# The fourth batch's first Fourier stage as quarter-size matmuls on sums and differences, with a new order of down matmuls around it

## Chip, core and metric

The kernel runs on one core of a Trainium2 chip. The metric is device microseconds of one execution. Five engines matter here. TensorE (PE in the profile) does the matmuls, VectorE (DVE) and ScalarE (ACT) do elementwise work and empty the PSUM banks that PE writes. GpSimd (POOL) and SyncE (SP) issue transfers (DMAs). Each engine works through its own instructions strictly in the order in which the kernel issues them, so an instruction that waits holds up all that stands behind it on that engine.

## The reference

```python
# x (8, 3008, 256), filt_r, filt_i (1505, 256)
X = np.fft.rfft(x, axis=1)
Y = X * (filt_r + 1j * filt_i)[None]
y = np.fft.irfft(Y, n=3008, axis=1).reshape(24064, 256)
h = y @ w_in                                       # (256, 2048)
g = np.maximum(h, 0.0) + alpha * np.minimum(h, 0.0)
out = g @ w_out                                    # (2048, 256)
```

A filter is applied in the frequency domain along the sequence, for each of 256 channels, and its result goes through two dense layers with a leaky rectifier between them.

## The kernel before

**The dense part.** The 24064 tokens are cut into 48 blocks of 512 tokens (the sixth of every twelve has 384). `Block.up` (L572) does, for one slice j of 128 of the 2048 hidden features, two matmuls of 512 columns ("U" below) into a PSUM tile `hps`, of which there are two. Two slices share one `hps` tile, so ScalarE empties a tile after every second step (L586). VectorE then forms `m` for each of the two slices (L589), and after every fourth step adds it to `gtb` (L591). `Block.down` (L626) multiplies the result with `w_out` ("down" matmuls, "d", 256 columns each, L631), a unit of four matmuls at a time (three in a block of 384), one block later than the ups. The queue `units` holds the units that are still to do. A PSUM tile `op` (two of them) holds the sums of 256 tokens. ScalarE copies it out (L636) and SyncE stores it (L559).

**The Fourier part.** 3008 is 94 times 32, and a batch goes through four stages, each cut into pieces. They work in float16.
- First stage: `piece_a` (L177, "A") multiplies a 94-row tile `xs` of the input with the table `wf1` of 96 columns: two matmuls of 512 columns into an `hps` tile, which ScalarE copies to `asb` (L313). There are eight pieces for a batch. `save_a` (L187) writes each quarter to `a_dram`, and `turn_a` (L221) reads it back with the axes turned, as `at`, both on SyncE's queue.
- Batches 4 to 7 (counted from 0) use another form of it. `load_halves` (L130) loads the first and the second half of the rows as two tiles `lo` and `hi`. `less` (L192) puts their difference beside them, in rows 64 to 110 of `lo`, and `plus` (L196) then overwrites the first rows with their sum; both are single VectorE instructions. `piece_q` (L200, "Q") does the same transform with four matmuls of 47 rows by 64 columns in the four quarters of the array, since the even outputs need the sum alone and the odd ones the difference alone.
- Second stage: `piece_b` (L231, "B"), eight matmuls of 64 rows by 64 columns into the single PSUM tile `psF`. VectorE multiplies it with two filter tables (L245 `ww`, L246 `uu`), GpSimd shifts `ww` between partitions by DMA into `sw` (L252), and `piece_s` (L255, VectorE L257) adds `sw` to `uu`. Batch 1 adds in the DMA instead (L250).
- Third stage: `piece_c` (L259, "C"), eight matmuls on `uu`, into an `hps` tile. Then a turn through DRAM again (L274).
- Fourth stage: `pair_d` (L303, "D"), eight matmuls of 94 columns into `psF`, emptied by ScalarE (VectorE in batch 0) into `yT`, which the ups read.

Batch 0 is done ahead of all by a class of its own (`First`, L321); its last pieces overlap the first block.

**The order of the work** is written out by hand. A step is one `up` of two matmuls. Blocks are 16 steps long; the first stepped block begins at step 16. `put` and `put_h` (L642, L645) enter pieces in a table `plan` by step, and `psum` counts at each step how many of them take an `hps` tile. The loop (L742 to L763) issues at each step first some downs (`pop`), then the planned pieces, then the two ups, then mostly one more unit of downs. Before step 150 one unit is popped ahead of planned pieces, where there are any. From step 150 on as many units as there are `hps` pieces are popped ahead of them and as many again behind them, and some odd steps keep their unit back so that there are enough (L759).

In batch 2 the pieces B stand at steps 106, 116, 126, 136, 148 and 158, the additions (`piece_s`) seven steps later, and the pieces C at 116, 126, 136, 148, 158 and 172 (L706). Batch 3's pieces A stand at 106, 112, 118, 124, 130, 132, 140 and 144 (L711). Its input tiles are loaded at steps 57, 69, 113 and 123, from a pool of four `xs` tiles.

**The lines of the tables** that the prediction uses: L184 A matmuls, L210 Q matmuls, L238 B, L269 C, L291 D, L577 and L600 ups, L631 downs; L313 all of ScalarE's copies from the Fourier stages; L194 `less`, L198 `plus`.

Of the kernel before, what the change touches and what calls it, by code (L numbers as in the profile page):

```python
# [15 lines left out]
N2 = 32  # L16
NK = 24
D = 256
# [37 lines left out]
def kernel(  # L56
# [56 lines left out]
        return bass.AP(tensor=x.tensor, offset=x.offset + (b * NFFT + 8 * c) * D,  # L113
                       ap=[[N2 * D, N1], [1, 8 * D]])

    def load_x(b, c, held=False):
        xs = p_x.tile([128, 8 * D], FP16, name="xs")
        if held:
            for r in (slice(0, 32), slice(64, 96)):
                nc.vector.memset(xs[r, 0:2], 0.0)  # L120
        if b:
            for r in (slice(0, 48), slice(48, N1)):
                nc.gpsimd.dma_start(out=xs[r], in_=xrow(b, c)[r])  # L123
        else:
            w = 8 * D // (1 + (c == 3))
            for o in range(0, 8 * D, w):
                nc.gpsimd.dma_start(out=xs[0:N1, o : o + w], in_=xrow(b, c)[:, o : o + w])
        return xs
# [37 lines left out]
    class Fft:  # L166
# [107 lines left out]
        def turn_c(self, q):  # L274
            k = 8 * q
            for par in range(2):
                for c in range(2):
                    r = par * 48 + c * NK + k
                    p = par * 64 + c * N2
                    nc.sync.dma_start(  # L280
                        out=v_dram[self.b, r : r + 8].rearrange("k s d -> s k d"),
                        in_=self.v[p : p + N2, k : k + 8])
            if q == 2:
                for g in range(4):
                    s = slice(8 * g, 8 * g + 8)
                    nc.sync.dma_start(out=self.zt[:, s], in_=v_dram[self.b, :, s])

        def inverse(self, pd, g, dh, mh):
# [278 lines left out]
    class Block:  # L567
        def __init__(self, p, t0, tn):
            self.p, self.t0, self.tn = p, t0, tn
            self.gts, self.gs = [], []  # L570

        def up(self, j):  # L572
            tn = self.tn
# [40 lines left out]
                nc.vector.tensor_add(g, g, m)  # L614
                self.gts += [g[:, h] for h in range(4)]

        def start_down(self, last):
            n = self.tn // 128
            ends = [2, 3, 4] if last else list(range(2, n, 2)) + [n]
            half = 12 if last else 8  # L620
            self.todo = []
            for s0, s1 in zip([0] + ends, ends):
                for ks in (range(half), range(half, 16)):
                    self.todo += [(s0, s1, si, k) for si in range(s0, s1) for k in ks]

        def down(self, q):  # L626
            n = self.tn // 128
            for s0, s1, si, k in self.todo[n * q : n * (q + 1)]:
                if si == s0 and k == 0:
                    self.op = psO.tile([128, 2, D], FP32, name="op")  # L630
                nc.tensor.matmul(self.op[:, si - s0], self.gts[k][:, 128 * si : 128 * si + 128],  # L631
                                 wout_s[:, k], start=(si == s0 and k == 0), stop=(si == s1 - 1 and k == 15))
                if k == 15 and si == s1 - 1:
                    m = s1 - s0
                    osb = p_osb.tile([128, 2, D], FP32, name="osb")
                    nc.scalar.activation(osb[:, 0:m], self.op[:, 0:m], AF.Copy)  # L636
                    for lane in range(m):
                        store(self.p, self.t0 + 128 * (s0 + lane), osb, lane)

# [2 lines left out]
    def put(step, fn, *args):  # L642
        plan.setdefault(step, []).append((fn, args))
# [4 lines left out]

    def plan_fft(b, a_at, ta, x_at, b_at, add, c_at, d_at):
        f = Fft(b)  # L650
        split = b > 3
        for q in range(6):
            put_h(c_at[q], f.piece_c, q)
            if q % 2 == 1:
                put(c_at[q] + 1, f.turn_c, q // 2)
        for q in range(6):
            put(b_at[q], f.piece_b, q, not add)
            if add:
                put(b_at[q] + add, f.piece_s, q)
        for i in range(8):  # L660
            put_h(a_at[i], f.piece_q if split else f.piece_a, i)
        for c in range(4):
            put(a_at[2 * c + 1] + split, f.save_q if split else f.save_a, c)
            if b in (2, 3):
                put(x_at[c], lambda b=b, c=c: xc.update({(b, c): load_x(b, c, b == 3 and c > 1)}))
            if split:
                x0, x1, x2 = x_at[c]
                put(x0, lambda b=b, c=c: xc.update({(b, c): load_halves(b, c)}))
                put(x1, f.less, c)
                put(x2, f.plus, c)  # L670
        w = NK // len(ta)
        for q, t in enumerate(ta):
            put(t, f.turn_a, nc.sync, w * q, w * q + w)
        for i in range(8):
            put(d_at[i], f.pair_d, i, on_act)
# [5 lines left out]
        nc.vector.tensor_scalar(alm_s, al_s, 1.0, -1.0, OP.mult, OP.add)  # L681

    put(1, f0.half_d, 1, on_act, "o")
    put(1, f0.half_d, 3, on_dve, "o")
    put(1, f0.piece_t, 2, on_dve)
    for i in (6, 7):
        put(3, lambda i=i: on_dve(*f0.half_t(i, "o")))
    put(7, f0.pair_d, 2, on_dve)
    for g, ts, ds, te, de in ((2, (19, 23), (26, 29), (on_dve, on_dve), (on_dve, on_dve)),
                              (3, (32, 34), (36, 38), (on_act, on_act), (on_act, on_act))):  # L690
        for i in range(2):
            put(ts[i], f0.piece_t, 2 * g + i, te[i])
            put(ds[i], f0.pair_d, 2 * g + i, de[i])
# [7 lines left out]
    def d_steps(p):  # L701
# [1 line left out]

    plan_fft(1, range(16, 32, 2), [31] * 4, None, (40, 46, 52, 58, 63, 68), 0, (52, 58, 64, 70, 76, 80),
             (93, 95, 98, 101, 114, 121, 142, 154))
    plan_fft(2, (48, 54, 60, 66, 72, 74, 82, 84), [90] * 4, (32, 40, 50, 56),  # L706
             (106, 116, 126, 136, 148, 158), 7, (116, 126, 136, 148, 158, 172), d_steps(96))
    for b in range(3, NB):
        p = 96 * (b - 1)
        if b == 3:  # L710
            a_at = (106, 112, 118, 124, 130, 132, 140, 144)  # L711
            x_at = (57, 69, 113, 123)
            ta = (155, 166)
        else:
            a_at = [p - 96 + t for t in (-34, -22, 2, 2, 14, 26, 38, 50)]
            x_at = [[p - 96 + t for t in r] for r in
                    ((-66 if b == 4 else -68, -52, -40), (-32, -18, -10), (-20, -4, 8), (4, 20, 32))]
            ta = (p - 39, p - 28)
        plan_fft(b, a_at, ta, x_at, range(p + 2, p + 74, 12), 8, range(p + 14, p + 86, 12), d_steps(p))

# [9 lines left out]
    for step in range(16):  # L730
# [4 lines left out]
                     8: [lambda i=i: f0.half_d(i, on_dve, "o") for i in (6, 7)]}.get(step, []))  # L735
        for fn, args in plan.pop(step, ()):
            fn(*args)
    blk.start_down(False)
    units.extend((blk, q) for q in range(16))
    step = 16  # L740

    for p, t0, tn in blocks[1:]:  # L742
        blk = Block(p, t0, tn)
        for j in range(16):
            n = psum.get(step, 0)
            if step < 150:
                pop(1 if n else 0)
            else:
                pop(n)
            for fn, args in plan.pop(step, ()):  # L750
                fn(*args)
            if step >= 150:
                pop(n)
            blk.up(j)
            if n:
                last = step
            else:
                soon = any(t in psum for t in range(step + 1, step + 14))
                if not (step >= 150 and step % 2 and step - last > 2 and soon and len(units) < 18 - j):  # L759
                    pop(1)  # L760
            step += 1
        blk.start_down(step == 16 * len(blocks))
# [33 lines left out]
```

## Time and profile before

| what | value |
|---|---|
| median of three runs | 768.38 us (768.12 to 769.5) |
| the profiled execution | 768.86 us, of which the span of the core is 767.1 us |
| granted TensorE clock | 1.0 |
| PE busy | 756.9 us, 99% of the span |
| DVE busy | 633.9 us, 83% |
| ACT busy | 583.3 us, 76% |
| POOL busy | 147.0 us, 19% |

Matmuls overlap in the trace: a busy matmul lasts longer than the distance to the next one. So the busy time says little about where PE loses time. What counts is the distance from one start to the next. Two ups of 512 columns stand 0.216 us apart, two downs 0.109 us. A larger distance is a stall, even if the profile calls only part of it idle. A view of a stretch of time lists the instructions of an engine merged by line, with the start, the length and, in square brackets, the idle time ahead of them and who ended it.

Step 16 begins at 43.9 us of the span, step 40 at 70.8, step 70 at 102.8, step 98 at 130.1, step 106 at 136.9, step 116 at 146.7, step 136 at 167.4 and step 158 at 188.6 (found by counting the U matmuls of the trace).

### The profile page before, as it was taken

The page shows a single profiled execution, that of the slowest core. Times are in us where ns is not written, and L with a number is a line of the kernel's source. Part 1 is how long each engine was busy: PE and PEld are TensorE (multiplying, and loading weights), DVE is VectorE, ACT ScalarE, POOL GpSimd, SP SyncE. Part 2 cuts the span into 40 slices and gives each one's busy share as a digit, 9 for nine tenths or more (in the row PEclk, how much of TensorE's full clock was granted, in tenths as well). Part 3 has the DMA queues.
Part 4 walks back from the last instruction along what each step waited for, and adds up shares of the span by engine and source line. Part 5 has one row for each costly group of instructions (what it writes and reads, how often), then busy time and mean ns, then how long its engine had stood idle before and what let it go on. Part 6 is the DMA issues. An engine that isn't in the chain of part 4 may idle for free.

```text
span 767.1 us, 16602 instructions
## 1 busy us (share of the span) xinstructions
PE 756.9 (99%) x6553; PEld 507.3 (66%) x6553; DVE 633.9 (83%) x1163; ACT 583.3 (76%) x672; POOL 147.0 (19%) x277
## 2 busy tenths in 40 slices
PE   8999999999999999999999999999999999999998
PEld 4666657666666666666666666766666666766666
DVE  4898975889889998899978998999877888666663
ACT  4788788888778777887778787787777777776664
POOL 6610840221211220121202122022101212000000
PEclk9999999999999999999999999999999999999999
DMA  9996996665752559533774438544463223510111
GB/s 162 157 225 173 175 204 181 166 171 139 178 153 69 139 142 197 143 97 97 188 205 96 125 104 179 166 97 118 131 162 87 71 68 97 152 36 28 42 42 56
DMA packets 97486, 100.04 MB, mean 130 GB/s; under 512 B 12086, under 2 KB 83398, under 8 KB 97216
## 3 DMA queue, kind: packets, MB, share of 16 engines
q1 hardware_dynamic: 82384, 69.50, 31.1%
q0 software_dynamic: 15024, 29.49, 21.4%
q8 instruction: 51, 0.84, 0.4%
q14 instruction: 27, 0.22, 0.1%
HBM read 55.02 MB, written 46.66 MB: 133 GB/s over the span
## 4 chain that ended last, share of the span: by engine, by line
PE 91%; DMA 4%; POOL 2%; DVE 1%; ACT 1%; issue 1%; SPq 0%; POOLq 0%; DVEq 0%; ACTq 0%
PE op L631 41%; PE hps L577 40%; PE psF L291 3%; PE hps L269 2%; PE psF L238 1%; PE hps L184 1%; DMA xs<-in_x_dram 1%; DMA uu<-ww 1%; PE hps L210 1%; DMA a_dram<-asb 1%; PE hps L600 1%; POOL filt_s L147 1%; DMA filt_s<-in_filt_r_dram 1%; POOL uu L250 1%; ACT asb L313 0%
## 5 line engine op out<-in xcount | busy, mean ns | idle before, releaser
L586 ACT ACTIVATE gtb<-hps 128x1024 f16<-128x1024 f32 (+1 forms) x376 | 377.9, 1007 | 132.6 <-PE hps L577 129.7
L631 PE MATMUL op<-wout_s,gtb 128*128 128x256 f16 x3008 | 431.1, 273 | 0.6 <-DVE gtb L614 0.6
L577 PE MATMUL hps<-yT,win_s 128*128 128x512 f16 (+1 forms) x1504 | 418.1, 375 | 0.3 <-ACT asb L313 0.2
L631 PEld LDWEIGHTS <-gtb 128*128 128x128 f16 x3008 | 290.8, 98 | 164.8 <-issue 10.7
L589 DVE TENSOR_SCALAR m<-gtb,alm_s 128x512 f16<-128x512 f16 (+1 forms) x752 | 227.3, 346 | 97.6 <-ACT gtb L586 96.1
L591 DVE TENSOR_TENSOR gtb<-gtb,m 128x2048 f16<-128x2048 f16 (+1 forms) x188 | 226.1, 1203 | 10.4
L577 PEld LDWEIGHTS <-win_s 128*128 128x128 f16 x1504 | 142.5, 98 | 54.9 <-issue 5.3
L252 POOL DMA_DIRECT2D sw<-ww x144 | 71.8, 506 | 414.2 <-DVE ww L245 399.4
L636 ACT ACTIVATE osb<-op 128x512 f32<-128x512 f32 (+1 forms) x97 | 56.6, 583 | 12.3 <-PE op L631 10.9
L313 ACT ACTIVATE asb<-hps 128x1024 f16<-128x1024 f32 (+1 forms) x56 | 56.7, 1020 | 6.4 <-PE hps L184 4.8
L245 DVE TENSOR_TENSOR ww<-psF,filts_s 128x1024 f16<-128x1024 f32 x42 | 51.2, 1219 | 1.0 <-DMA uu<-ww 0.7
L313 ACT ACTIVATE v<-hps 128x1024 f16<-128x1024 f32 (+1 forms) x43 | 43.5, 1012 | 11.2 <-PE hps L269 11.1
L246 DVE TENSOR_TENSOR uu<-psF,filt_s 128x1024 f16<-128x1024 f32 x42 | 51.1, 1216 | 0.0
L313 ACT ACTIVATE yT<-psF 128x752 f16<-128x752 f32 (+1 forms) x59 | 46.5, 788 | 1.7 <-PE psF L291 1.5
L291 PEld LDWEIGHTS <-zt 96*128 96x128 f16 x504 | 28.0, 98 | 5.8 <-issue 0.4
L291 PE MATMUL psF<-wi_s,zt 96*128 96x94 f16 x448 | 27.9, 205 | 0.0
L257 DVE TENSOR_TENSOR uu<-uu,sw 128x1024 f16<-128x1024 f16 x36 | 24.6, 683 | 1.3 <-DMA sw<-ww 1.3
L250 POOL DMA_DIRECT2D uu<-ww x24 | 19.6, 1174 | 28.1 <-DVE uu L246 21.4
L123 POOL DMA_DIRECT2D xs<-in_x_dram x24 | 17.6, 1009 | 12.9 <-DMA win_s<-in_moe_w_in_dram 4.5
L194 DVE TENSOR_TENSOR xs<-xs 47x2048 f16<-47x2048 f16 x16 | 19.5, 1219 | 0.4
L198 DVE TENSOR_TENSOR xs<-xs 47x2048 f16<-47x2048 f16 x16 | 19.4, 1210 | 0.0
L269 PE MATMUL hps<-uu,twi_s 64*64 64x256 f16 x336 | 17.6, 281 | 0.2 <-DMA uu<-ww 0.2
(99 smaller groups left out, 264.8 us busy)
## 6 DMA issues: line engine op xcount, KB each, us to landing
out_dram<-osb SPq DMA_DIRECT2D x128, 128.0 KB
v_dram<-v SPq DMA_DIRECT2D x84, 128.0 KB
zt<-v_dram SPq DMA_DIRECT2D x28, 384.0 KB
sw<-ww POOLq DMA_DIRECT2D x144, 64.0 KB, 2.7
xs<-in_x_dram POOLq DMA_DIRECT2D x40, 192.0 KB, 6.6
at<-a_dram SPq DMA_DIRECT2D x40, 192.0 KB
a_dram<-asb SPq DMA_DIRECT2D x32, 192.0 KB
a_dram<-asb SPq DMA_DIRECT2D x12, 384.0 KB
```

Of the source, the lines that this page charges most:

```text
L245: nc.vector.tensor_mul(ww, px, fs)
L246: nc.vector.tensor_mul(uu, px, f)
L252: nc.gpsimd.dma_start(out=sw[o : o + 32], in_=ww[i : i + 32])
L269: nc.tensor.matmul(ps[64 * par : 64 * par + 64, e, 256 * h : 256 * h + 256], twi_s[r, 4 * q + 2 * h + par], u[r, par, h], start=True, stop ...
L291: nc.tensor.matmul(ps[:, m], self.zt[:, 8 * g + 4 * mh + m, dh * 128 : dh * 128 + 128], self.wi, start=True, stop=True)
L313: nc.scalar.activation(o, i, AF.Copy)
L577: nc.tensor.matmul(self.hps[:, j % 2, 0:tn], win_s[:, kt, j * 128 : (j + 1) * 128], yT[:, kt, self.t0 : self.t0 + tn], start=(kt == 0), st ...
L586: nc.scalar.activation(g[:, 2 * i : 2 * i + 2], self.hps[:, :, 0:tn], AF.Copy)
L589: nc.vector.tensor_scalar(m[:, 2 * i + h], g[:, 2 * i + h], 0.0, a, OP.min, OP.mult)
L591: nc.vector.tensor_add(g, g, m)
L631: nc.tensor.matmul(self.op[:, si - s0], self.gts[k][:, 128 * si : 128 * si + 128], wout_s[:, k], start=(si == s0 and k == 0), stop=(si == ...
L636: nc.scalar.activation(osb[:, 0:m], self.op[:, 0:m], AF.Copy)
```

## The change

- Batch 3 joins batches 4 to 7 in the quartered first stage (`split = b > 2`). Its pieces Q stand at steps 98, 98, 106, 106, 116, 126, 136 and 148. For each of the four input tiles the load, `less` and `plus` stand at (69, 80, 86), (91, 98, 102), (99, 108, 112) and (107, 122, 130). The two small memsets of the earlier loads go.
- The rule of downs on both sides of the planned pieces holds from step 96 on rather than 150.
- The first stepped block's downs (of block 0) go by quarters of k: the first four k of all four token groups, then the next four, so that two `op` tiles are open at once. At step 16 no unit is popped ahead of the piece, at step 24 two are.
- In batch 0 the turn `whole_t(2)` is issued on PE ahead of `half_d(3)` and emptied behind it; the second of the turns of group 2 moves from step 23 to 24 and the two D pieces of that group from 26 and 29 to 27 and 30.
- Batch 2's loads are entered at steps 39, 45, 51, 57 rather than 32, 40, 50, 56, and batch 4's first load one step later. Batch 3's `zt` is read in eight transfers rather than four.

In the order of issue, GpSimd's queue changes only by batch 3's loads: its first one no longer stands ahead of the transfers of batch 1's fourth piece B (step 58), and the two first ones now stand behind those of the sixth (step 68).

```diff
-    def load_x(b, c, held=False):
+    def load_x(b, c):
         xs = p_x.tile([128, 8 * D], FP16, name="xs")
-        if held:
-            for r in (slice(0, 32), slice(64, 96)):
-                nc.vector.memset(xs[r, 0:2], 0.0)
...
             if q == 2:
-                for g in range(4):
-                    s = slice(8 * g, 8 * g + 8)
+                w = 4 if self.b == 3 else 8
+                for g in range(0, N2, w):
+                    s = slice(g, g + w)
                     nc.sync.dma_start(out=self.zt[:, s], in_=v_dram[self.b, :, s])
...
-        def start_down(self, last):
+        def start_down(self, last, quarters=False):
             n = self.tn // 128
+            if quarters:
+                self.todo = [(s0, s0 + 2, si, k) for k0 in range(0, 16, 4) for s0 in range(0, n, 2)
+                             for si in (s0, s0 + 1) for k in range(k0, k0 + 4)]
+                return
...
-        split = b > 3
+        split = b > 2
...
-            if b in (2, 3):
-                put(x_at[c], lambda b=b, c=c: xc.update({(b, c): load_x(b, c, b == 3 and c > 1)}))
+            if b == 2:
+                put(x_at[c], lambda b=b, c=c: xc.update({(b, c): load_x(b, c)}))
...
     put(1, f0.half_d, 1, on_act, "o")
+    put(1, lambda: later.append(f0.whole_t(2)))
     put(1, f0.half_d, 3, on_dve, "o")
-    put(1, f0.piece_t, 2, on_dve)
+    put(1, lambda: on_dve(*later.pop()))
...
-    for g, ts, ds, te, de in ((2, (19, 23), (26, 29), (on_dve, on_dve), (on_dve, on_dve)),
+    for g, ts, ds, te, de in ((2, (19, 24), (27, 30), (on_dve, on_dve), (on_dve, on_dve)),
...
-    plan_fft(2, (48, 54, 60, 66, 72, 74, 82, 84), [90] * 4, (32, 40, 50, 56),
+    plan_fft(2, (48, 54, 60, 66, 72, 74, 82, 84), [90] * 4, (39, 45, 51, 57),
...
-            a_at = (106, 112, 118, 124, 130, 132, 140, 144)
-            x_at = (57, 69, 113, 123)
+            a_at = (98, 98, 106, 106, 116, 126, 136, 148)
+            x_at = ((69, 80, 86), (91, 98, 102), (99, 108, 112), (107, 122, 130))
...
-                    ((-66 if b == 4 else -68, -52, -40), (-32, -18, -10), (-20, -4, 8), (4, 20, 32))]
+                    ((-65 if b == 4 else -68, -52, -40), (-32, -18, -10), (-20, -4, 8), (4, 20, 32))]
...
-    blk.start_down(False)
+    blk.start_down(False, True)
...
-            if step < 150:
-                pop(1 if n else 0)
+            if step < 96:
+                pop({16: 0, 24: 2}.get(step, 1 if n else 0))
...
-            if step >= 150:
+            if step >= 96:
                 pop(n)
...
-                if not (step >= 150 and step % 2 and step - last > 2 and soon and len(units) < 18 - j):
+                if not (step >= 96 and step % 2 and step - last > 2 and soon and len(units) < 18 - j):
                     pop(1)
```

In `down`, `self.op` becomes a table by `s0`, so that both open tiles are found.

## The prediction

> **What bounds the kernel now.** I read the page's busy row first, then PE's waits, then the distances from start to start of PE's matmuls.
>
> ```profile
> PE 756.9 (99%) x6553; PEld 507.3 (66%) x6553; DVE 633.9 (83%) x1163; ACT 583.3 (76%) x672; POOL 147.0 (19%) x277
> ```
>
> ```profile
> PE op L631 <- DVE gtb L614: 0.6, 2, 0.4
> PE psF L238 <- DMA at<-a_dram: 0.2, 1, 0.2
> PE hps L269 <- DMA uu<-ww: 0.2, 1, 0.2
> ```
>
> PE is the bound. Its waits are few, and longer than listed, since a busy matmul is drawn longer than its share: the C piece at step 70 starts at 103.79 and goes on at 104.31, a stall of 0.51 us where the list says 0.2. Summed by distances, PE stalls some 9.6 us in the run, 6.0 of them ahead of 45 us, and 0.3 in four places between steps 106 and 146. So a change gains by less PE work or by these stalls, and loses by each new one.
>
> **The change, part by part.** Times are of the profiled execution. Ahead of step 98 I count gains as a shift of all engines.
>
> *PE work.* Two stretches of PE's timeline, with C and B alone and with Q behind them:
>
> ```profile
> 147.61 0.41 PE L269 MATMUL hps<-uu,twi_s 64*64 64x256 f16 x8
> 147.86 0.39 PE L238 MATMUL psF<-at,twf_s 64*64 64x256 f16 x8
> 148.18 1.04 PE L577 MATMUL hps<-yT,win_s 128*128 128x512 f16 x4
> ```
>
> ```profile
> 190.01 0.41 PE L269 MATMUL hps<-uu,twi_s 64*64 64x256 f16 x8
> 190.26 0.39 PE L238 MATMUL psF<-at,twf_s 64*64 64x256 f16 x8
> 190.47 0.39 PE L210 MATMUL hps<-xs,wfq_s 47*64 47x512 f16 x4
> 190.79 1.05 PE L631 MATMUL op<-wout_s,gtb 128*128 128x256 f16 x8
> ```
>
> From C to what follows takes 0.57 us without Q and 0.78 with it: Q costs 0.21 to 0.22 in such a burst. A costs 0.43 (172.45 to 172.88 at step 140). Six Q stand behind B: 6 x 0.22 = 1.31 less. The two at step 98 stand alone and pay for entering and leaving the small tiles, 0.09 each: the last down stands 0.20 ahead of C at 190.01, not 0.109. So 0.87 becomes 0.62. Sum: **-1.56**. The four stalls between 106 and 146 go with A: **-0.30**.
>
> [...]
>
> *Start.* At 33.64 PE waits 0.49 for an `op` tile (`half_d(3)`); the eight turn matmuls, 0.45, go into that hole, so PE and ScalarE run 0.44 earlier. Before, downs wait for `gtb` at 43.05 (0.38) and 45.36 (0.56). With no unit at step 16, A follows the last up4 at 42.23, but the ups wait for `hps`, which ScalarE empties until 43.45: 0.8 lost. The downs at 44.37 need the first quarter alone, ready at 42.55. A of step 18 then starts at 45.24 instead of 46.25, with one unit (0.44) owed: 0.57 ahead. At step 27 D arrives at 56.15, and the `zt` copy, now behind an add in VectorE's queue, ends at 56.35: 0.25 back. **-0.32**, between 0 and -0.57.
>
> *Step 70.* GpSimd issues batch 3's first loads at 92.03 and 92.53, between `ww` and the shifts for that C; the last shift is issued at 96.15 and takes 8.1 us, against 5.5 for the median. Without them the stall goes: **-0.50**, between 0 and that. The 0.52 at 71.30 stays: those reads follow `asb` of step 30, which only moves along.
>
> *ScalarE at steps 98 to 106.* This is how two Q in a row look, at step 290:
>
> ```profile
> 314.35 0.60 PE L210 MATMUL hps<-xs,wfq_s 47*64 47x512 f16 x8
> 314.79 1.94 ACT L313 ACTIVATE asb<-hps 128x1024 f16<-128x1024 f32 x2 [0.15 <-PE hps L210]
> 314.88 0.83 PE L631 MATMUL op<-wout_s,gtb 128*128 128x256 f16 x6
> 315.86 1.02 PE L577 MATMUL hps<-yT,win_s 128*128 128x512 f16 x4 [0.15 <-ACT asb L313]
> ```
>
> Q fills an `hps` tile in 0.22, ScalarE needs 0.92 from one to the next, and six downs (0.65) don't cover the rest: the up at 315.86 is 0.31 late. Step 98 has the same with D ahead, whose copy (0.70) goes first: with the step beginning at 130.10, the copy starts at 131.23, `asb` at 131.93, ends at 132.95, and the ups wait from 132.38 to 133.00: 0.62. ScalarE's backlog, with D's copy of step 101, delays the ups of 104 by 0.31 and, behind an `osb` copy, those of 106 by 0.50. **+1.43**, between 0.6 (twice 0.31) and 1.8.
>
> [...]
>
> *VectorE, steps 106 to 136.* Here is its queue in the same stretch, before:
>
> ```profile
> 138.98 1.22 DVE L245 TENSOR_TENSOR ww<-psF,filts_s 128x1024 f16<-128x1024 f32 x1
> 140.11 1.22 DVE L246 TENSOR_TENSOR uu<-psF,filt_s 128x1024 f16<-128x1024 f32 x1
> 141.24 0.63 DVE L589 TENSOR_SCALAR m<-gtb,alm_s 128x512 f16<-128x512 f16 x2
> 141.91 1.22 DVE L591 TENSOR_TENSOR gtb<-gtb,m 128x2048 f16<-128x2048 f16 x1
> 143.05 1.26 DVE L589 TENSOR_SCALAR m<-gtb,alm_s 128x512 f16<-128x512 f16 x4
> 144.35 1.23 DVE L591 TENSOR_TENSOR gtb<-gtb,m 128x2048 f16<-128x2048 f16 x1
> 145.49 0.68 DVE L257 TENSOR_TENSOR uu<-uu,sw 128x1024 f16<-128x1024 f16 x1
> ```
>
> It has no gap from B's products (step 106) to the addition of step 113, which C of step 116 needs: the addition ends at 146.17, C starts at 147.52. The margin is 1.35. The change puts `less` of step 108 and `plus` of 112 ahead of that addition: 1.14 us each from start to start (later batches' rows of L194 and L198), 2.28. Followed through from step 98: VectorE idles until 135.08, when ScalarE delivers the late `gtb` of steps 98 and 99; then products, adds and `plus` of 102 put `ww` at 141.15; 2.26 for `ww` and `uu`, 1.8, `less` 1.14, 2.43, `plus` 1.13 and the addition's 0.68 end at 150.6. PE reaches C at 148.55, since it too lost 1.43. **+2.1**. The ten steps up to 126 add one `less` and VectorE just keeps up (addition at 160.5, C at 160.7). Up to 136 they add a `plus` to a full queue: addition at 171.0, PE there at 170.1: **+0.95**. From 136 to 148 nothing is added, and the wait ends. Bounds of both together: 0, if VectorE is ahead somewhere, and 5, if `less` of 108 also waits for its load.
>
> *At nothing:* `less` and `plus` of steps 80 and 86, since VectorE is busy only 11.2 of 20.1 us between 110.0 and 130.1 (without that cover, up to 2.3); the four more `zt` issues (0.42 each on SP's row) and four more `asb` writes, since batch 3's D follow 17 steps later; the other loads, whose place in GpSimd's order stays, and which are issued as soon as a tile is free, not at their step. If SP fell behind, the stores of `osb` would hold ScalarE, about 0.6 each.
>
> Sum: -1.56 - 0.30 - 0.32 - 0.50 + 1.43 + 2.1 + 0.95 = **+1.8 us**: 768.86 becomes 770.7. The median lies 0.48 below the profiled execution, so 768.38 becomes **770.2 us**.
>
> **Rivals.**
> 1. *VectorE is in time.* If the addition of 113 ends by 148.55, no C waits and 3.05 goes: 767.1. For it: VectorE's 17% of idle time. Against: its gapless rows above, with 1.35 of margin against 2.28 of added work.
> 2. *The other side: ScalarE is hidden too.* If the six downs behind the doubled Q cover its copies, because ScalarE starts step 98 with no backlog, 1.43 goes as well: 765.7. It decides at one point: whether the first `asb` ends within 0.65 of the last Q. Against: 0.31 late at step 290, and there no D copy stood ahead.
> 3. *The queue stays late.* If `less` of 108 waits for its load, or B of 116 finds `psF` not emptied, two more us are lost: 772.2. The loads took 6.6 us (median of the page) and have over 10 here; that speaks against it.
>
> That Q doesn't run four at a time can be left out: the rows show it.
>
> **Numbers.** Chances: forecast 0.50, first rival 0.25, second 0.10, third 0.15. A difference under 0.2% (1.54 us) can't be told from none. A third of the forecast's case falls below that on the slow side, and a third of the first rival's beyond it on the fast side: faster 0.18, same 0.34, slower 0.48. The range, 766.8 to 772.2, takes in the first rival and half of the third. Alone, the forecast's case spans 769.0 to 771.5.
>
> **What would show it.** C of step 116 late behind L257's successor by about 2 us, and of 136 by 1; an up of L577 late behind `asb` at steps 98, 104 and 106; no stall at step 70's C; L631 no longer waiting for `gtb` of L614; 32 Q matmuls more and 16 A less. If VectorE shows gaps between steps 106 and 113, the forecast's main step is wrong. If PE stalls at neither 98 nor 116, the change is faster by about 0.35%.

## The result, and the profile after

The changed kernel takes 776.39 us in the median of six runs (772.46 to 780.92), against 768.38 us for the kernel before. The ratio is 1.0098, with a 95% interval of 1.0073 to 1.0122: it is slower by 1.0%. The direction is that of the forecast; the size is not. The forecast was 770.2 us, and 776.39 lies 4.2 us above the upper end of the range.

The profiled execution of the changed kernel took 775.0 us, of which the span is 773.2 us. The page's busy row:

```profile
PE 757.5 (98%) x6569; PEld 507.1 (66%) x6569; DVE 642.8 (83%) x1167; ACT 583.2 (75%) x672; POOL 146.3 (19%) x277
```

PE is busy for 0.6 us longer than before in a span that is 6.1 us longer. So PE mostly waits for the difference, or works more slowly. The changed kernel's line numbers are shifted by two or three: C is L266, B L235, D L289, Q L207, the ups are L575, the downs L633, the addition is L254, `less` L191, `plus` L195, and ScalarE's copy of the Fourier stages L311. The waits of PE (in total, number, longest):

```profile
PE hps L266 <- DVE uu L254: 2.8, 2, 2.1
PE psF L289 <- DMA zt<-v_dram: 2.6, 1, 2.6
...
PE hps L575 <- ACT asb L311: 0.7, 2, 0.5
```

The first is the wait of C for the addition that the prediction had, in two places. The third is that of the ups for ScalarE. The second, D waiting for its `zt` tile, isn't in the prediction. The waits of the downs for `gtb` (0.6 us in two places before) are gone, as foreseen.

**C of step 116.** PE's timeline:

```profile
149.33 1.04 PE L633 MATMUL op<-wout_s,gtb 128*128 128x256 f16 x8
152.51 0.41 PE L266 MATMUL hps<-uu,twi_s 64*64 64x256 f16 x8 [2.14 <-DVE uu L254]
152.76 0.39 PE L235 MATMUL psF<-at,twf_s 64*64 64x256 f16 x8
152.97 0.39 PE L207 MATMUL hps<-xs,wfq_s 47*64 47x512 f16 x4
153.29 1.89 PE L633 MATMUL op<-wout_s,gtb 128*128 128x256 f16 x8
154.98 1.89 PE L575 MATMUL hps<-yT,win_s 128*128 128x512 f16 x4
```

By starts the stall is 2.21 us. The last two rows show something else: eight downs take 1.69 us from start to start of what follows, where 0.87 is usual (eight times 0.109), and four ups 1.70 instead of 0.86. VectorE's timeline up to that addition:

```profile
142.90 1.22 DVE L242 TENSOR_TENSOR ww<-psF,filts_s 128x1024 f16<-128x1024 f32 x1
144.04 1.22 DVE L243 TENSOR_TENSOR uu<-psF,filt_s 128x1024 f16<-128x1024 f32 x1
145.17 0.63 DVE L587 TENSOR_SCALAR m<-gtb,alm_s 128x512 f16<-128x512 f16 x2
145.84 1.23 DVE L589 TENSOR_TENSOR gtb<-gtb,m 128x2048 f16<-128x2048 f16 x1
147.09 1.22 DVE L191 TENSOR_TENSOR xs<-xs 47x2048 f16<-47x2048 f16 x1
148.33 1.14 DVE L587 TENSOR_SCALAR m<-gtb,alm_s 128x512 f16<-128x512 f16 x4
149.51 1.22 DVE L589 TENSOR_TENSOR gtb<-gtb,m 128x2048 f16<-128x2048 f16 x1
150.65 1.21 DVE L195 TENSOR_TENSOR xs<-xs 47x2048 f16<-47x2048 f16 x1
151.78 0.68 DVE L254 TENSOR_TENSOR uu<-uu,sw 128x1024 f16<-128x1024 f16 x1
```

No row has an idle time ahead of it: it is the full queue of the prediction, with `less` (147.09) and `plus` (150.65) in it.

**D of step 93.** Before, D started at 125.88 without a wait of note. In the changed kernel's timeline, all engines, the rows that matter (SPq and POOL rows are issues of transfers) are:

```profile
117.08 2.11 SPq L277 DMA_DIRECT2D v_dram<-v  x4
...
118.59 0.62 POOL L131 DMA_DIRECT2D xs<-in_x_dram  x1 [7.77 <-PE hps L181]
...
122.05 0.52 POOL L129 DMA_DIRECT2D xs<-in_x_dram  x1 [2.84 <-DVE xs L195]
...
122.65 2.78 SPq L284 DMA_DIRECT2D zt<-v_dram  x4
...
124.30 0.60 PE L633 MATMUL op<-wout_s,gtb 128*128 128x256 f16 x4
...
127.46 0.51 PE L289 MATMUL psF<-wi_s,zt 96*128 96x94 f16 x8 [2.56 <-DMA zt<-v_dram]
```

The same of the kernel before, from the rows of GpSimd, SyncE and PE:

```profile
109.53 2.12 POOL L123 DMA_DIRECT2D xs<-in_x_dram  x2
118.10 2.12 SPq L280 DMA_DIRECT2D v_dram<-v  x4
122.14 1.73 SPq L286 DMA_DIRECT2D zt<-v_dram  x4
125.88 0.51 PE L291 MATMUL psF<-wi_s,zt 96*128 96x94 f16 x8
146.73 1.03 POOL L123 DMA_DIRECT2D xs<-in_x_dram  x2 [4.26 <-issue]
```

The reads of `zt` wait until the writes of `v` have landed, as SyncE's waits between 116 and 128 us of the changed kernel show (in total, number, longest):

```profile
SPq L284 <- DMA v_dram<-v: 3.3, 2, 2.1
```

From the first write to the first read it took 4.04 us before (118.10 to 122.14) and takes 5.57 now (117.08 to 122.65); from the first read to D's start, 3.74 before and 4.81 now. Two input loads of GpSimd, at 118.59 and 122.05, run beside these transfers: the second half of batch 3's second quarter (c = 1) and the first half of its third. In the kernel before, GpSimd issues no input load between 111.6 and 146.7.

**The clock.** The busy time in stretches of the changed kernel; the third number from the end is the clock that was granted:

```profile
core 0: us, PE busy (x) PEld busy (x) DVE busy (x) ACT busy (x) POOL busy (x), PEclk, DMA share, GB/s
149.90:153.31 3.41, 1.27 (x26) 0.67 (x24) 3.41 (x7) 0.99 (x2) 0.00 (x0) 1.00 0.74 192
153.31:156.72 3.41, 3.41 (x17) 1.77 (x14) 3.38 (x4) 1.61 (x2) 0.52 (x2) 0.50 0.04 12
```

Right behind the stall PE runs for 3.41 us at half clock. Half the work of that time, 1.7 us, is lost, beside the stall itself.

**The account of the profiled execution**, by distances between starts:

| term | forecast | measured |
|---|---|---|
| Q for A, the four stalls after 106, start, C of step 70 | -2.68 | no stall at C; ups of 16 late by 0.78, D of 27 by 0.29, as forecast; the rest not measured alone |
| ups of steps 98, 104, 106 | 0.62, 0.31, 0.50 | 0.65, 0.34, 0.40 |
| C of steps 116 and 136 | 2.1, 0.95 | 2.21, 0.74 |
| D of step 93 (0.06 before) | 0 | 2.73 |
| half clock behind step 116 | 0 | 1.7 |

With the forecast's -2.68, the sum is -2.68 + 1.39 + 2.95 + 2.67 + 1.7 = +6.0. Measured: 775.0 - 768.86 = +6.1. Taken the other way, the measured terms leave -2.6 for the first line, which was forecast as -2.68; it is a remainder and was not measured by itself.

The runs spread with their mean clock: 772.46 us at 1.0, 774.29 and 775.0 at 0.998, 777.78 at 0.996, 777.94 and 780.92 at 0.993. One half-clock stretch of 3.41 us lowers the mean by 0.0022, so 0.993 is about three of them, some 5 us. The slowest run is 8.5 us above the fastest, and the rest of that distance isn't explained here.

### The profile page after: what moved, and what is told of

Read it like the earlier page. It is cut to its first block, busy times and chain, and to the rows that moved or that the text cites. A ratio compares the mean times of both kernels' runs of the same rounds, so it can differ in the third digit from the quotient of the medians.

```text
span 773.2 us, 16643 instructions
## 1 busy us (share of the span) xinstructions
PE 757.5 (98%) x6569; PEld 507.1 (66%) x6569; DVE 642.8 (83%) x1167; ACT 583.2 (75%) x672; POOL 146.3 (19%) x277
## 4 chain that ended last, share of the span: by engine, by line
PE 88%; DVE 5%; DMA 3%; ACT 1%; POOL 1%; issue 1%; SPq 0%; DVEq 0%; ACTq 0%; POOLq 0%
PE op L633 40%; PE hps L575 39%; PE psF L289 3%; PE hps L266 2%; PE psF L235 1%; DVE m L587 1%; DMA xs<-in_x_dram 1%; PE hps L207 1%; DVE gtb L589 1%; DVE gtb L612 1%; DMA zt<-v_dram 1%; PE hps L598 1%; DVE m L611 1%; POOL filt_s L144 1%; ACT asb L311 1%
## 5 line engine op out<-in xcount | busy, mean ns | idle before, releaser
L633 PE MATMUL op<-wout_s,gtb 128*128 128x256 f16 x3008 | 431.4, 273 | 0.0
L575 PE MATMUL hps<-yT,win_s 128*128 128x512 f16 (+1 forms) x1504 | 418.0, 375 | 1.9 <-ACT asb L311 0.7
L633 PEld LDWEIGHTS <-gtb 128*128 128x128 f16 x3008 | 290.9, 98 | 164.0 <-issue 13.0
L575 PEld LDWEIGHTS <-win_s 128*128 128x128 f16 x1504 | 143.1, 98 | 57.0 <-issue 7.7
L311 ACT ACTIVATE asb<-hps 128x1024 f16<-128x1024 f32 (+1 forms) x56 | 56.4, 1020 | 5.0 <-PE hps L181 3.4
L311 ACT ACTIVATE v<-hps 128x1024 f16<-128x1024 f32 (+1 forms) x43 | 43.5, 1011 | 14.3 <-PE hps L266 14.2
L311 ACT ACTIVATE yT<-psF 128x752 f16<-128x752 f32 (+1 forms) x59 | 46.5, 787 | 4.4 <-PE psF L289 4.2
L289 PEld LDWEIGHTS <-zt 96*128 96x128 f16 x504 | 28.0, 98 | 8.8 <-DMA zt<-v_dram 2.8
L289 PE MATMUL psF<-wi_s,zt 96*128 96x94 f16 x448 | 27.9, 205 | 2.6 <-DMA zt<-v_dram 2.6
L254 DVE TENSOR_TENSOR uu<-uu,sw 128x1024 f16<-128x1024 f16 x36 | 24.6, 682 | 2.0 <-DMA sw<-ww 1.9
L191 DVE TENSOR_TENSOR xs<-xs 47x2048 f16<-47x2048 f16 x20 | 24.4, 1220 | 1.4 <-DMA xs<-in_x_dram 0.9
L195 DVE TENSOR_TENSOR xs<-xs 47x2048 f16<-47x2048 f16 x20 | 24.2, 1209 | 0.0
L266 PE MATMUL hps<-uu,twi_s 64*64 64x256 f16 x336 | 17.3, 281 | 2.8 <-DVE uu L254 2.8
L235 PE MATMUL psF<-at,twf_s 64*64 64x256 f16 x336 | 16.5, 272 | 0.0
```

What stands on the lines that cost most here:

```text
L266: nc.tensor.matmul(ps[64 * par : 64 * par + 64, e, 256 * h : 256 * h + 256], twi_s[r, 4 * q + 2 * h + par], u[r, par, h], start=True, stop ...
L289: nc.tensor.matmul(ps[:, m], self.zt[:, 8 * g + 4 * mh + m, dh * 128 : dh * 128 + 128], self.wi, start=True, stop=True)
L311: nc.scalar.activation(o, i, AF.Copy)
L575: nc.tensor.matmul(self.hps[:, j % 2, 0:tn], win_s[:, kt, j * 128 : (j + 1) * 128], yT[:, kt, self.t0 : self.t0 + tn], start=(kt == 0), st ...
L633: nc.tensor.matmul(self.op[s0][:, si - s0], self.gts[k][:, 128 * si : 128 * si + 128], wout_s[:, k], start=(si == s0 and k == 0), stop=(si ...
```

## The experiments

My theory after the result: the loss over the forecast comes from the two loads of batch 3's second and third quarter, which start at 118 to 122 us and delay D of step 93, and from half-clock stretches that a stall brings about. The rivals: the sums on VectorE cost more than the stall they make; the new rule of downs from step 96 on is at fault; the start is. Each comparison below was made beside runs of the kernel before on the same chip, whose medians were 768.8 us.

**1. No sums in the third quarter.**

```diff
+        if (b, c) == (3, 2):
+            hi = lo[64:112]
-                put(x1, f.less, c)
-                put(x2, f.plus, c)
+                if (b, c) != (3, 2):
+                    put(x1, f.less, c)
+                    put(x2, f.plus, c)
```

> The changed kernel, but for the third quarter of batch 3's input (entered at steps 108 and 112) VectorE forms neither difference nor sum: the second half of the rows is loaded straight into rows 64 to 111, so batch 3's result lacks them. Two instructions of 1.14 us each leave VectorE's queue between the products of step 106 and the addition of step 113; nothing else moves. Theory (C of step 116 waits for VectorE's queue, and the half clock for 3.4 us behind it follows from that idle time): the wait of 2.2 us at C of step 116 falls to about 0, the half clock behind it goes, the stall of 2.7 us at D of step 93 stays. Times without any half clock about 770, the median nearer to that than to 776. Rival (C waits for the shifts by DMA, not for VectorE): the wait stays at about 2 us and the median at about 776.

Measured: 773.5 us (770.02 to 775.69), ratio 1.0057 [1.0038, 1.0076]. The median was expected nearer to 770. C of step 116 is late by 0.87 instead of 2.21, not by 0. VectorE's timeline shows that something else is late next:

```profile
150.54 1.23 DVE L591 TENSOR_TENSOR gtb<-gtb,m 128x2048 f16<-128x2048 f16 x1
152.74 0.69 DVE L256 TENSOR_TENSOR uu<-uu,sw 128x1024 f16<-128x1024 f16 x1 [0.97 <-DMA sw<-ww]
```

VectorE now idles 0.97 us ahead of the addition, for the shift of `ww`. So `less` and `plus` make the stall, but without them the path through ScalarE's lateness, B, `ww` and the shift leaves 0.87. D of step 93 is 3.72 late here, with a third load beside the turn (118.32, 122.16 and 122.67), since this quarter takes one tile rather than two. The clock is halved right behind it (129.03 to 132.44). The time fell by 2.9 us, more than the 1.34 of the stall, and the rest stays within the spread that the clock makes.

**2. Holding the loads.** A memset on a tile at the time its load is entered keeps the load from being issued before VectorE gets there (in the last run of the two, GpSimd's load at 128.25 has waited 17.52 us for it). First for the second half of the second quarter alone, then for both halves.

```diff
+        if (b, c) == (3, 1):
+            nc.vector.memset(hi[0:32, 0:2], 0.0)
-            x_at = ((69, 80, 86), (91, 98, 102), (99, 108, 112), (107, 122, 130))
+            x_at = ((69, 80, 86), (95, 98, 102), (99, 108, 112), (107, 122, 130))
```

> The changed kernel, but the load of the second half of batch 3's second quarter waits for a tiny memset that VectorE does at step 95, so that it and the load queued behind it start behind D of step 93 and not at 118 to 125 us, beside the writes and reads of batch 1's turn. Theory (these two loads delay the zt reads): the stall at D of step 93 falls from 2.7 us to under 0.3, as in the kernel before (0.06), and C of step 116 waits as before or up to 1 us longer, since the difference of step 98 may wait for its load; about 2 us less than the changed kernel at the same clock, so some 770 to 770.5 without half clock, and half clock at C of 116 still in some executions. Rival (the zt reads are late because SyncE's queue is behind, with its stores and writes): the stall stays at 2 us or more.

Measured: 774.34 us (772.61 to 775.88), ratio 1.0068 [1.0057, 1.008]. D of step 93 is late by 0.75, more than expected, and one load still began at 120.42. It began 2.33 us behind the first write of `v`, and the reads followed the writes after 4.00 us, as without a load; it is the distance from the first read to D that is long, 5.23 against 3.74. C of step 116 is 2.21 late as before.

```diff
+        if (b, c) == (3, 1):
+            for t in (lo, hi):
+                nc.vector.memset(t[0:32, 0:2], 0.0)
```

The second quarter is entered at step 95 here as well.

> The changed kernel, but both loads of batch 3's second quarter wait for tiny memsets of VectorE at step 95, so that no input load at all runs between 111 us and D of step 93. In the run with one of them held, one load still began at 120.4 and the stall at D was 0.75 us. Theory (input loads beside batch 1's turn delay the zt reads): the stall at D of step 93 falls under 0.3 us. C of step 116 waits as before, 2.2 us. Without half clock about 770, with one stretch of it 771.7; median 770 to 772. Rival (something else than the loads is left): the stall stays near 0.75.

Measured: 773.28 us (771.91 to 775.72), ratio 1.0055 [1.0037, 1.0073], above the 770 to 772 that I expected. SyncE's and GpSimd's rows of its timeline:

```profile
117.49 2.11 SPq L280 DMA_DIRECT2D v_dram<-v  x4
121.51 1.72 SPq L287 DMA_DIRECT2D zt<-v_dram  x4
```

```profile
128.25 0.52 POOL L132 DMA_DIRECT2D xs<-in_x_dram  x1 [17.52 <-DVE xs L131]
128.75 0.52 POOL L134 DMA_DIRECT2D xs<-in_x_dram  x1
```

With the loads at 128.25 the writes take 4.02 us to the first read again, as in the kernel before, and D is late by 0.08. This shows the cause: the loads. Three more kernels below hold both loads. Their writes take 4.00 to 4.03 us as well, but D is late by 0.15 (experiment 9), 0.51 (experiment 8) and 1.12 (the one with a filler at step 116), so some tenths, and once a whole microsecond, come from elsewhere. In the last of these the stores ahead of the writes on SyncE's queue took 3.15 us rather than 2.37. (What stands behind the held load in GpSimd's queue, the third quarter's load of 122.05, is held too: it goes out at 129.26.) The hold has its own price: the second Q of step 106 waits 0.73 for its sums, and C of step 116 is 2.76 late.

**3. Fillers in the stalls.** Matmuls that nothing reads keep PE busy where it would wait: between 125 and 128 us PE is busy for 2.94 us with them, and for 0.54 in the changed kernel.

```diff
+    put(93, lambda: warm(12, banks(False)[:, 0]))
+    put(116, lambda: warm(10, banks(False)[:, 0]))
```

> The changed kernel with dummy matmuls of 512 columns that nothing reads, 12 ahead of D at step 93 and 10 ahead of C at step 116: PE works through 2.6 and 2.2 us in which it else stood still. Theory (idle time of PE within one window of 3.4 us makes the half clock, by chance of where the window lies): mean clock 1.0 in every execution, the times within 1 us of each other, about 772.5 (the lowest time of the changed kernel, which had clock 1.0). Rival (the half clock has another cause, such as the quartered matmuls or the load): clock between 0.993 and 0.998 in most executions, and a median at 776 or above.

Measured: 774.34 us (773.9 to 777.76), ratio 1.0082 [1.0066, 1.0097]. The clock is 0.999 or 1.0 in five of six runs. The median lies some 2 us above the expected time, which was the lowest of the changed kernel's six runs. The fillers were not longer than the stalls: in the profile D starts 0.22 us and C of step 116 0.14 us behind the end of the last filler. A new wait of 0.64 at C of step 158 is a part of the 2 us; the rest isn't shown. As a cure the fillers are of little use; as a test of the clock they worked. With the loads held as well (the edit above, and fillers at step 116 alone):

> The kernel with both loads of the second quarter held until step 95, and ten dummy matmuls that nothing reads ahead of C of step 116. Theory (idle time within one window makes the half clock; only C of step 116 still has enough of it): clock 0.999 to 1.0 in every execution, times within 1.5 us of each other, median about 770.5. Rival (half clock by chance of the chip or by the quartered matmuls): 0.998 or lower in half of the executions, as without the filler.

Measured: 772.12 us (771.28 to 773.42), ratio 1.0038 [1.0025, 1.0052], clock 0.999 or more in all eight runs. The clock came as expected. The median is 1.6 us above the expected 770.5; in the profile D of step 93 is 1.12 late, the second Q of step 106 waits 0.8, and C of step 116 starts 0.7 behind its filler.

**4. The start alone,** put into the kernel before: downs by quarters, the turn ahead of `half_d(3)`, the moved pieces.

> The kernel before with the start of the change alone: the turn ahead of half_d(3), group 2's pieces at 24, 27 and 30, downs by quarters of k, no unit at step 16 and two at 24. Theory: the downs at 43 to 46 us wait no more, the ups of step 16 wait 0.8 us, D of step 27 waits 0.3; 0.3 us less, 768.1, hardly told from none. Rival (the start costs, since two op tiles are open and ScalarE's copies bunch): 0.5 us or more slower.

Measured: 768.36 us in 11 runs, ratio 0.9995 [0.9986, 1.0004]. The ups of step 16 wait 0.78 and D of step 27 0.29, as in the changed kernel. The gain of 0.45 can't be told from none, and the start isn't the loss. With the loads of batch 3 behind the shifts as well:

```diff
-            x_at = (57, 69, 113, 123)
+            x_at = (69, 70, 113, 123)
```

> The kernel before with the start of the change and with batch 3's first input load entered at step 69 rather than 57, so that it stands behind the shifts of batch 1's last pieces B on GpSimd's queue; batch 3 keeps its undivided first stage. Theory: the stall at C of step 70 (0.5 us before, 0.7 in the run with the start alone) goes, and with the start's 0.4 the time is 0.9 us under the kernel before, about 767.8. Rival (the shift is late by chance of the transfers, not by the load ahead of it): the stall stays, 768.4.

Measured: 768.84 us in 12 runs, ratio 1.0004 [0.9991, 1.0016]. The stall of C at step 70 is gone, as the prediction had it, and D of step 93 is 0.77 late in its place. So the -0.50 of step 70 is real as a stall but wasn't kept. The four loads were issued at 108.4 to 110.0 and took 7.5 to 9.9 us to land, so the last of them still ran when the writes of `v` began at 117.46, and those took 4.67 us to the first read.

**5. ScalarE's copies of D to VectorE** (batch 1's third and fourth).

```diff
-            put(d_at[i], f.pair_d, i, on_act)
+            put(d_at[i], f.pair_d, i, on_dve if (b, i) in ((1, 2), (1, 3)) else on_act)
```

> The changed kernel with the copies of batch 1's D pieces of steps 98 and 101 done by VectorE rather than ScalarE. Theory (ScalarE's queue of D copy and two asb copies holds the ups): the up of step 98 is 0.65 us late in the changed kernel and under 0.1 here, that of step 104 0.34 and under 0.1; C of step 116 within 0.5 of its 2.2, since VectorE idles at step 98. The total gains up to 0.9, which the spread of the half clock hides. Rival (the ups wait for something else, or the doubled Q alone fills both tiles): 0.3 or more is left at step 98.

Measured: 777.41 us (776.74 to 779.79), ratio 1.0111 [1.0093, 1.0129]. The ups of step 98 are late by 0.36 instead of 0.65. I had expected under 0.1, and that was wrong: two Q in a row leave 0.3 by themselves, which the prediction had read from step 290. D's copy makes only the other 0.3. Those of step 104 fall from 0.34 to 0.08. VectorE pays: C of step 116 is 2.69 late.

**6. The old rule of downs.** The number 96 goes back to 150 in the three conditions of the loop.

> The changed kernel with the old rule of downs: one unit ahead of planned pieces until step 150, none behind them and none kept back. Theory (the units behind the pieces cover ScalarE): the up of step 98 waits 1.2 us or more rather than 0.65, that of 106 about 1.0 rather than 0.4, and the ups of 116 to 148 0.2 to 0.5 each; 1 to 3 us slower than the changed kernel at the same clock, 773.5 to 775.5 without half clock. Rival (the new rule is itself the loss, since it leaves steps without downs): 1 us or more faster than the changed kernel.

Measured: 776.21 us (774.2 to 777.43), ratio 1.0097 [1.0081, 1.0113]: about the median of the changed kernel. The stalls are others. Two rows of PE's timeline, the ups of steps 98 and 106:

```profile
135.37 1.02 PE L575 MATMUL hps<-yT,win_s 128*128 128x512 f16 x4 [1.24 <-ACT asb L311]
143.80 1.02 PE L575 MATMUL hps<-yT,win_s 128*128 128x512 f16 x4 [0.99 <-ACT asb L311]
```

By starts they are about 1.3 and 1.1 late (0.65 and 0.40 in the changed kernel), as expected, and the ups of 116, 126, 136 and 148 wait 0.69 to 0.86 each, more than expected. In all, PE waits 5.1 us for ScalarE between 130 and 200 us, against 0.9 in the changed kernel. D of step 93 is 3.51 late. C of step 116, which PE reaches later, is only 0.88 late, and C of step 136 doesn't wait. No half clock follows in the profiled execution, and the three runs at clock 1.0 took 774.2, 774.64 and 776.21 us, against 772.46 in the only such run of the changed kernel. So the new rule isn't the loss. It takes away waits for ScalarE, and at equal clock it seems to gain 2 to 4 us, about 0.8 of which is the later D; the half clock hides this in the medians.

**7. The kernel before with three VectorE operations,** whose result nothing reads, ahead of the addition of step 113.

```diff
+    def extra():
+        t = p_m.tile([128, 4, 512], FP16, name="m")
+        for _ in range(3):
+            nc.vector.tensor_tensor(t[0:47].rearrange("p a b -> p (a b)"), win_s[0:47, 0], win_s[0:47, 1], OP.add)
+
+    put(112, extra)
```

> The kernel before with three additions of 47 x 2048 elements, whose result nothing reads, ahead of the addition of step 113 on VectorE. No quartered piece and no other load is in it. Theory (C of step 116 has a margin of 1.35 us against VectorE's queue, and the half clock needs idle time alone): 3 x 1.14 - 1.35 = 2.1 us of wait at C of step 116; 2.1 us slower at full clock, 770.9, and in a third to a half of the executions a stretch of half clock, 1.7 more. Rival for the wait (the shifts by DMA set it): under 0.5 us. Rival for the clock (it needs the quartered matmuls): clock 0.999 or 1.0 in all.

Measured: 772.2 us (771.48 to 774.54), ratio 1.0057 [1.0043, 1.007]. Its VectorE, and then its clock:

```profile
146.86 3.71 DVE L707 TENSOR_TENSOR m<-win_s 47x2048 f16<-47x2048 f16 x3
150.50 0.68 DVE L257 TENSOR_TENSOR uu<-uu,sw 128x1024 f16<-128x1024 f16 x1
```

```profile
147.91:151.32 3.41, 1.24 (x14) 0.78 (x15) 3.26 (x6) 1.02 (x1) 0.00 (x0) 1.00 0.15 52
151.32:154.74 3.42, 3.42 (x25) 1.66 (x26) 3.36 (x6) 1.65 (x2) 1.11 (x2) 0.50 0.51 72
```

The three take 3.64 us from start to start, and C of step 116 is 2.24 late: 3.64 less the margin of 1.35 that the prediction had found gives 2.29. The half clock stands right behind the stall here too, in a kernel that has none of the change. So margin and clock are both shown without it.

**8. The second quarter held, and no sums in the third** (experiments 1 and 2 together).

> The changed kernel with both edits that took a stall away, together: the loads of batch 3's second quarter held until step 95, and for the third quarter neither difference nor sum is formed (the second half of the rows is loaded in their place, so batch 3's result lacks them). Theory (the two stalls and the half clock behind them are the whole loss beyond what ScalarE costs): D of step 93 waits 0.1 to 1.1 us, C of step 116 under 0.9, clock 0.999 to 1.0 in nearly every execution, median 769 to 770.5. Rival (another loss is hidden behind these): median at 772 or above.

Measured: 769.55 us in 12 runs, ratio 1.0015 [1.0002, 1.0029]; the clock is 0.999 or 1.0 in eleven of them. With D late by 0.51, C of step 116 by 0.63 and the second Q of step 106 by 0.23, nearly all of the 8 us is gone. So the loads, VectorE's queue and the clock behind their stalls made up the loss, in a kernel that leaves out one difference and one sum.

**9. The sums on GpSimd,** which is busy for 19% of the span, with the second quarter held.

```diff
-            nc.vector.tensor_tensor(lo[64:111], lo[0:47], hi[0:47], OP.subtract)
+            (nc.gpsimd if self.b == 3 else nc.vector).tensor_tensor(lo[64:111], lo[0:47], hi[0:47], OP.subtract)
```

(and the same for the sum.)

> The changed kernel with the second quarter's loads held until step 95 and with batch 3's differences and sums formed by GpSimd rather than VectorE. Theory (VectorE's queue makes C wait): C of step 116 waits under 0.9 us, of 136 under 0.3; how long GpSimd takes for one is shown by no run so far; if under 2 us, Q of step 106 waits up to 2 us and the total is 768.5 to 771, if 4 us or more, Q of 106 and the shifts queued behind wait longer and it is 773 or above. Rival: C of 116 waits 2 us as before.

Measured: 792.22 us (791.14 to 793.51), ratio 1.0311 [1.0298, 1.0325]. GpSimd's timeline:

```profile
136.36 4.17 POOL L194 TENSOR_TENSOR xs<-xs 47x2048 f16<-47x2048 f16 x1 [4.60 <-DMA xs<-in_x_dram]
140.48 0.57 POOL L132 DMA_DIRECT2D xs<-in_x_dram  x1
141.04 0.52 POOL L134 DMA_DIRECT2D xs<-in_x_dram  x1
141.63 4.80 POOL L198 TENSOR_TENSOR xs<-xs 47x2048 f16<-47x2048 f16 x1
148.28 2.00 POOL L252 DMA_DIRECT2D sw<-ww  x4 [1.84 <-DVE ww L245]
```

A sum takes 4.04 to 4.8 us there, against 1.22 on VectorE. The Q of step 106 waits 7.9 us for it. C of step 116 is 7.0 late and a later one 3.5: the shifts (148.28) stand in the same queue behind the sums. Behind these stalls PE ran at half clock, in all some 20.5 us of the span of 790.2, worked out from the mean clock of 0.987.

No version here was faster than the kernel before by more than its interval.

## Why the prediction was right in most of its steps and wrong in its size

- **What bounds the kernel**: right. Everything that was lost was lost on PE.
- **PE work, start**: nothing speaks against -1.56, which wasn't measured alone. From C to what follows Q takes 0.78 at steps 116, 126 and 136, as read from step 158. The start's pieces came as worked out (0.8 and 0.25 forecast, 0.78 and 0.29 measured), and its whole can't be told from none.
- **Step 70**: the stall went, as said, by the place in GpSimd's queue. What it gives was not kept when done by itself (experiment 4). Nor could 0.5 be seen there: from the first up of step 40 to that of step 80 the kernel before took 43.0 us, and the ten kernels that are the changed one up to there took 42.5 to 44.5, since in some of them other C wait for their shifts.
- **ScalarE at steps 98 to 106**: right, 1.43 against 1.39, and with the old rule of downs the same ups wait for ScalarE longer (experiment 6).
- **VectorE, steps 106 to 136**: right, 3.05 against 2.95. The gapless rows and the margin of 1.35 carried it, and experiment 7 gave the margin a second time.
- **The step that failed** is the line "At nothing", in its words "the other loads, whose place in GpSimd's order stays, and which are issued as soon as a tile is free, not at their step". Both halves are true, and the price was wrong. I never asked when a tile is free. A quarter now takes two of the pool's four tiles, where it took one. So the second half of the second quarter, which went out with the first at 109.53 before, has to wait until A of step 84 releases its tile, and goes out at 118.59. The first half of the third goes out at 122.05, when `plus` of step 86 releases its tile. In the kernel before, the small memset on its tile had held the third quarter's load until VectorE reached step 113, and it went out at 146.73; that memset is gone. So both loads fall into the turn of batch 1. Cost: 2.7 us at D of step 93 (2.9 to 3.7 in other kernels with the same loads, 0.08 to 1.12 in the four with both held). No kernel here brings back that memset alone, so what each of the two changes costs isn't shown.
- **A term was missing**: what a stall does to the clock. 1.7 us for each half-clock stretch, one in the profiled execution, none to about three in others. It makes up a good part of the spread from 772.5 to 780.9. Without these two, the profiled execution would be 6.1 - 2.7 - 1.7 = +1.7 us, against +1.8 forecast: the terms that were in the sum were right, and two were not in it.
- **Rivals**: the first two (VectorE in time, ScalarE hidden) didn't come. The third had the right sign by luck: its named causes, `less` waiting for its load or `psF` not emptied, didn't come: no idle time stands ahead of `less` at 147.09.

## What to carry to other kernels

Where an edit takes away something that holds a transfer back, or makes it need more buffers, work out from the trace when its buffer now comes free, and which transfers on the critical path run at that time; "its place in the queue stays" is no answer. Stalls of PE of 2.21 us (the changed kernel), 2.24 (experiment 7), 2.76 (both halves held) and 3.72 (experiment 1) were followed by half clock, and others of 2.21 (second half held), 2.73 (the changed kernel) and 3.51 (experiment 6) were not. So in this kernel such a stall has to be priced, by chance, at 1.7 us or more above its length (experiment 5 has two half-clock windows behind one stall of 2.87 us), and a forecast with such a stall needs a wider range. Nearly full queues are forecast well by writing out their rows with the new work in place: 2.1 became 2.21, 0.95 became 0.74.

## What the runs showed of the hardware

**Stretches of one clock lasted 3.413 us or a multiple of it.** The changed kernel's record of the clock has 146.77 us at full speed, then 3.413 at half clock, then 617.81 at full speed; the two longer ones are 43 and 181 times 3.413. So the windows below are counted in steps of 3.413 us from a record of the clock; where the clock doesn't change at a border, the border is counted and not seen. Windows of an execution with a stall and what came next, by views like the one above:

| kernel, window | PE busy in it | clock of the next window |
|---|---|---|
| after, 149.90 to 153.31 | 1.27 | 0.5 |
| experiment 7, 147.91 to 151.32 | 1.24 | 0.5 |
| both halves held (experiment 2), 149.59 to 153.00 | 1.39 | 0.5 |
| no sums (experiment 1), 125.62 to 129.03 | 0.85 | 0.5 |
| D's copies on VectorE (experiment 5), 124.13 to 127.54 | 1.38 | 0.5 |
| second half held (experiment 2), 148.65 to 152.06 | 1.58 | 1.0 |
| old rule of downs (experiment 6), 126.37 to 129.78 | 1.59 | 1.0 |
| after, 126.00 to 129.42 | 1.96 | 1.0 |

The rows of the old rule, whose D stalls for 3.51 us across a border:

```profile
122.96:126.37 3.41, 1.88 (x16) 1.25 (x13) 2.73 (x6) 0.82 (x2) 0.06 (x1) 1.00 0.77 147
126.37:129.78 3.41, 1.59 (x18) 1.27 (x19) 0.00 (x0) 1.04 (x2) 0.00 (x0) 1.00 1.04 259
129.78:133.20 3.42, 3.42 (x36) 2.56 (x34) 1.52 (x5) 3.02 (x5) 0.00 (x0) 1.00 0.98 302
```

Here 3.51 us of stall cost no half clock, and neither window was left with less than 1.59 us of work. The 2.21 us at step 116 did, when they fell inside one window and left 1.27. So in these eight windows the busy time tells the two outcomes apart, with half clock behind 0.85 to 1.39 us of 3.41 and full clock behind 1.58 to 1.96, and the length of the gap does not. What comes behind a busy time between 1.39 and 1.58, and what holds for other matmuls, isn't shown. At half clock, a busy window need not end it: experiment 5's window of 127.54 to 130.95, at half clock and busy for 2.73 us, was followed by half clock again, while one of experiment 9 with 2.99 (146.07 to 149.48) was followed by full clock. Halved, these are 1.37 and 1.50: the first lies among the windows with half clock behind them, the second between the two groups, so that the same border would fit all ten if work done is what counts. That is an estimate from two windows.

**Input loads beside a turn.** From the first write of `v` to the first read it takes 5.57 us in the changed kernel, whose load starts 1.5 us behind the first write, and 6.15 and 6.07 in experiments 1 and 6, with the same load. In the kernel before and with both halves held (experiment 2), where no load is issued in that time, it takes 4.04 and 4.02. Which part of the transfer is shared isn't shown here.
